# The expert stage of an attention and mixture-of-experts kernel: work order from a list scheduler, low parts of the weights on VectorE, threshold products on the whole array

## The chip, the cores and the metric

The kernel runs on one core of one Trainium2 chip. The metric is the device time of one execution in microseconds (us); the kernel before has a median of 897.88 us over three runs (896.49 to 899.35). The engines are named as the profile names them: PE is TensorE (PEld its weight loads), DVE is VectorE, ACT is ScalarE, POOL is GpSimd, and SP is the engine that issues most DMAs.

## The reference

Linear attention over 8 batches, 8 heads, 576 positions of 64 features feeds a mixture of eight experts over all 4,608 tokens of 512 features. Only the second half matters here:

```python
def _moe_ref(x, w_gate, w1, w2):
    N, D = x.shape; E = w_gate.shape[1]; cap = N // E          # 4608, 512, 8, 576
    logits = x @ w_gate
    order = np.argsort(-logits.flatten())
    # walk all (token, expert) pairs from the highest logit down: a token goes to
    # the first expert that still has room (cap tokens each)
    ...
    for e in range(E):
        mask = assigned == e
        h = np.maximum(x[mask] @ w1[e], 0.0)                   # [576,512] @ [512,1024]
        out[mask] = h @ w2[e]                                  # [576,1024] @ [1024,512]
```

## The kernel before, in words

**Two stages.** The attention stage fills DRAM with the token rows (`xs`) and SBUF with the logits (`L`). Its order comes from a list scheduler, class `Plan`: each piece of work is added with an engine, a duration, a due time and the pieces it needs, and `order()` repeatedly takes the piece that can start first. The change does not alter what the attention stage puts into it. The expert stage, function `moe`, follows.

**Routing.** For the expert that fills up next, `routing(r)` finds which of the eight it is and the 576 tokens that it takes. It fixes the cut-off logit digit by digit. A digit is a chain between DVE and PE: DVE compares every token with 32 or 64 thresholds (`cmp`, L549, bf16), PE counts per expert (L563, nine or eighteen small products of 128 rows), DVE picks the counts (`mm`, `dd`, L564 and L566), PE sums them with `Q` (L568, a product of 32 or 64 columns), DVE tests them against the capacity (`fl`, L571), PE spreads the flags with a matrix of ones (L573, a product over 32 or 64 rows), and DVE reads off the digit and forms the next remainder (`ch`, `cc`, L574 and L578). Six digits make a threshold. Then the expert's number `ei` is known, the taken tokens are ranked (L605, L606) and put into a table (L628, L633, L652), from which `idx`, the list of rows, is written (L654 to L657). At last the logits of what was taken are struck out (L661 to L669). The next expert's `prep` (L465 to L492) needs those logits. So the routing of eight experts is one long chain. Expert 0's routing stands in front of all matmuls; the later ones run beside the experts' matmuls. Expert 7's has no digits, since it gets what is left.

**An expert.** POOL gathers its 576 token rows with five indirect DMAs (`gather`, L675). PE transposes them (L710); ACT copies the result as the high part `xh` (L711) and DVE forms the low part `xl` (L702). All large products are made of three products of rounded 32-bit numbers: high with high, high with low, low with high. The weights come as eight raw chunks of 128x1024 (`wraw`, DMAs on SP), ACT rounds each to its high part (L692), and POOL subtracts it to get the low part (`w1l`, `w2l`, L693; one single chunk of the first expert is done on DVE). Layer 1 (`l1`, L729) is 16 groups of 12 products of 272 or 304 columns; ACT and DVE split each into `fh` and `fl`. Layer 2 (`l2`) is four blocks of 24 products of 512 columns (L747) and a last block of 64 tokens straight from the raw 32-bit weights, which uses only 64 columns of the array (L756). ACT copies each block and POOL scatters it to the output (L760, L761).

**What sets the order.** The expert stage is written out by generators. `l1w` and `l2w` yield after every few products, `run` counts a model time, and `rstep` puts the next step of the routing in when its due time, set by constants such as `lat0`, `latd` and `slack`, has come. The weight chunks and the transposes of the next expert hang at fixed places in those loops. Each engine then works through its own row in order, and an instruction that waits for another engine holds up all that stand behind it in its row.

Of the kernel before, what the change touches and what calls it, by code (L numbers as in the profile page):

```python
# [17 lines left out]
class Plan:  # L18
# [3 lines left out]
    SEM=40.  # L22
    def __init__(self,stay=0.): self.t=[]; self.by={}; self.stay=stay
    def add(self,name,eng,dur,due,fn,deps=(),lat=0.,mode=None,slot=None,frees=(),after=0.):

        x=dict(name=name,eng=eng,dur=dur,due=due,fn=fn,deps=list(deps),lat=lat,mode=mode,slot=slot or (),frees=frees,after=after,n=len(self.t))
        self.t.append(x); self.by[name]=x
    def order(self):
# [7 lines left out]
        while left:  # L36
            best=None; horizon={}
            cand={}
            for x in left:
# [29 lines left out]
            s,x=pick; e=x['eng']
            if e=='PE':  # L70
                if mode[0] not in (None,x['mode']): s+=95.
                if mode[0]!=x['mode'] or s>free.get(e,0.)+1.: s+=100. if x['mode']=='A' else 50.
                mode[0]=x['mode']
            x['start']=s; free[e]=s+x['dur']; x['end']=s+x['dur']+x['lat']
# [307 lines left out]
def moe_consts(rp, nc, C, L, MC, cfg={}):  # L382
# [45 lines left out]
    for n in (2,4):  # L428
        ir=ident.rearrange('p (k i) -> p k i',i=n)
        m=rp.tile([128,n,8],F32,name=f'msk{n}'); q=rp.tile([128,128//n],F32R,name=f'Q{n}')  # L430
# [4 lines left out]
        with nc.allow_low_precision(reason='zeros and ones'): V.tensor_reduce(q.rearrange('p (k o) -> p k o',o=1),ir,axis=AX.X,op=OP.max)  # L435
# [4 lines left out]
    for i in range(2): V.tensor_copy(dup[:,i,:],Q[2])  # L440
# [69 lines left out]
def moe(ctx, tc, nc, L, xs, w1, w2, out, C, MC, R0, cfg={}):  # L510
# [17 lines left out]
    def routing(r):  # L528
# [3 lines left out]
        if not last:  # L532
            R=R0 if r==0 else state()
            if r:
                for x in prep(R,0,NT): yield x
            dg,OH=R['dg'],R['OH']
            c=dg[:,0]; lat=cfg.get('lat0',1.2)
            for i,(sh,bits) in enumerate(DIG):
# [15 lines left out]
                yield lat+.9*K/32  # L554
# [5 lines left out]
                else:  # L560
                    p=rps([128,n,8])
                    for g in range(NT//n):
                        PE.matmul(p,cmp[:,g].rearrange('p k i -> p (k i)'),OH[:,g*n:g*n+n,:],start=g==0,stop=g==NT//n-1)  # L563
                    mm=S([128,n,8],f'mm{n}'); V.tensor_mul(mm,p,msk[n])  # L564
                    dd=S([128,8,1],'dd',F32R)
                    with nc.allow_low_precision(reason='whole numbers under 2**13'): V.tensor_reduce(dd,mm.rearrange('p i e -> p e i'),axis=AX.X,op=OP.add)  # L566
                    yield cfg.get('lq',.9)
                    p=rps([K,8]); PE.matmul(p,Q[n],dd[:,:,0],start=True,stop=True)  # L568
# [3 lines left out]
                yield cfg.get('lo',.6)  # L572
                p=rps([128,8]); PE.matmul(p,ones[0:K],fl,start=True,stop=True)  # L573
# [4 lines left out]
                V.scalar_tensor_tensor(c2,c,ch,dg[:,i+1],op0=OP.subtract,op1=OP.add); c=c2  # L578

# [23 lines left out]
        yield cfg.get('latr',1.6) if not last else cfg.get('lat7',1.5)  # L603
        p=rps([128,2])
        PE.matmul(p,tri,tot,start=True,stop=False)  # L605
        PE.matmul(p[:,1:2],low,tot[:,0:1],start=False,stop=True)  # L606
        off=S([128,2],'off'); V.tensor_copy(off,p)
# [8 lines left out]
        yield -1.3  # L616
# [6 lines left out]
        yield -.9  # L623
# [6 lines left out]
        yield cfg.get('latc',1.6)  # L630
        p=rps([128,9,2,2])
        for g in range(18):
            PE.matmul(p,lo[:,g].rearrange('p k i -> p (k i)'),hv[:,g],start=g==0,stop=g==17)  # L633
        idx=S([128,6,1],'idx',I32,b=3)
        if wide:

            pb=S([128,9,2,2],'pb',BF); V.tensor_copy(pb,p)
            yield cfg.get('lm',.9)
# [5 lines left out]
        else:  # L644
# [14 lines left out]
        if not last:  # L659
            yield -.4  # L660
# [10 lines left out]
    def gather(r):  # L671
        xg=fp.tile([128,5,Dm],F32,name='xg',bufs=cfg.get('bxg',1))
        T['xg',r]=xg
        for b,(o,n) in enumerate(BL):
            G.indirect_dma_start(out=xg[0:n,b,:],out_offset=None,in_=xs,in_offset=bass.IndirectOffsetOnAxis(ap=T['idx',r][0:n,b,:],axis=0))  # L675
    W={}
    def wreg(r):
        W['e',r]=nc.sync.value_load(T['ei',r][0:1,0:1],min_val=0,max_val=E-1)
    def wraw(name,r,c):
        e=W['e',r]; src=w1 if name=='w1' else w2  # L680
        raw=fp.tile([128,4,256] if name=='w1' else [128,2,512],F32,name='raw'+name,bufs=4)
        if name=='w1':
            s=src[ds(e,1)].rearrange('o (k p) f -> p (o k) f',p=128)[:,:,256*c:256*c+256]
        else:
            s=src[ds(e,1)].rearrange('o (k p) f -> p (o k) f',p=128)[:,2*c:2*c+2,:]
        nc.sync.dma_start(raw,s)
        W[name,r,c]=raw
    def wconv(name,r,c,eng=None):
        raw=W[name,r,c]
        h=fp.tile(list(raw.shape),F32R,name=name+'h',bufs=4)  # L690
        l=fp.tile(list(raw.shape),F32R,name=name+'l',bufs=4)
        A.copy(h,raw)  # L692
        (eng or G).tensor_sub(l,raw,h)  # L693
        W[name,r,c]=(h,l,raw)
    def wchunk(name,r,c): wraw(name,r,c); wconv(name,r,c)
    SC=[]
    LQ=[]
    def lag(t,f,*a,**k): LQ.append((st['now']+t,st['lab'],f,a,k))
    def flush(t):
        while LQ and LQ[0][0]<=t:  # L700
            _,lab,f,a,k=LQ.pop(0)
            f(*a,**k)  # L702
    def xt(r,lg=None):
        lg=cfg.get('lgx',.9) if lg is None else lg
        xh=fp.tile([128,4,cap],F32R,name='xh',bufs=1); xl=fp.tile([128,4,cap],F32R,name='xl',bufs=1)
        T['xt',r]=(xh,xl)
        for b,(o,n) in enumerate(BL):
            p=ps.tile([128,4,128],F32,name='h',bufs=cfg.get('hb',4))
            for k in range(4):
                PE.transpose(p[:,k,0:n],T['xg',r][0:n,b,128*k:128*k+128],ident[0:n,0:n])  # L710
            A.copy(xh[:,:,o:o+n],p[:,:,0:n])  # L711
            lag(lg,V.tensor_sub,xl[:,:,o:o+n],p[:,:,0:n],xh[:,:,o:o+n])
            yield .45
    def l1(r,so=False):
        if not so: flush(1e9)
        xh,xl=T['xt',r]
        hh=fp.tile([128,8,512],F32R,name='fh',bufs=1); hl=fp.tile([128,8,512],F32R,name='fl',bufs=1)
        hf=fp.tile([128,8,cap-512],F32,name='ff',bufs=1)
        T['h',r]=(hh,hl,hf)
        SP=(0,cfg.get('hc',288),cap)  # L720
        for i in range(16):
                f,s=(i%8,i//8) if so else (i//2,i%2)
                c,o=f//2,(f%2)*128
                w1h,w1l,_=W['w1',r,c]
                p=ps.tile([128,4,128],F32,name='h',bufs=cfg.get('hb',4))
                o1,o2=SP[s:s+2]; p=p.rearrange('p a b -> p (a b)')[:,0:o2-o1]
                n=0
                for xx,ws,k in [(xh,ws,k) for k in range(4) for ws in (w1h,w1l)]+[(xl,w1h,k) for k in range(4)]:
                    PE.matmul(p,ws[:,k,o:o+128],xx[:,k,o1:o2],start=n==0,stop=n==11); n+=1  # L729
                    if n in (3,6,9): yield .365  # L730
                m1=min(o2,512)-o1
# [164 lines left out]
```

## Time and profile before

| | |
|---|---|
| median of the runs | 897.88 us |
| the profiled execution | 900.97 us, of which the span from its first to its last instruction is 899.1 us |
| mean granted TensorE clock | 0.976 |
| PE busy over the span | 844.9 us (94%) |
| DVE busy | 591.6 us (66%) |
| POOL busy | 425.0 us (47%) |
| ACT busy | 387.1 us (43%) |
| bytes moved by DMA | 91.63 MB |

The first transpose of expert 0 starts at 399.49 us, so the attention stage and the first routing take some 400 us and the expert stage the other 500. A time line row reads: start, duration, engine, line, operation, what it writes and reads, shape, count, and in brackets how long the engine had been idle before it and what ended that idle time. Consecutive matmuls overlap, so what one costs is the distance between two starts, not the duration.

### The profile page before, as it was taken

The numbers are of one execution on the slowest core, as the hardware profiler recorded it, in microseconds if no ns is written. First come the engines' busy times: TensorE is split into PE (matmuls) and PEld (weight loads), VectorE is DVE, ScalarE is ACT, GpSimd is POOL, SyncE is SP. The second block draws the span as 40 slices with busy tenths as digits, with TensorE's granted clock in tenths as the row PEclk, the third lists the DMA queues.
The fourth block names the chain that finished last, engine by engine and source line by source line (L and its number), as shares of the span: only waits on it lengthen the run. The fifth ranks groups of instructions, "written<-read, shape, count | busy, mean of one in ns | idle before, by whom it ended". The sixth has DMA issues, their size and how long they took to land.

```text
span 899.1 us, 20953 instructions
## 1 busy us (share of the span) xinstructions
PE 844.9 (94%) x8332; PEld 728.9 (81%) x8332; DVE 591.6 (66%) x1655; ACT 387.1 (43%) x836; POOL 425.0 (47%) x399
## 2 busy tenths in 40 slices
PE   7999999999999999658989999999999899999995
PEld 5788888888888888657768869869779788798894
DVE  7798898889889988667765665655656645520210
ACT  3556666666566666322323324333333233343420
POOL 2945655555454444043273463553642734665321
PEclk9999999999999999759999999999999999999998
DMA  9534444444444400142133241440531331550301
GB/s 193 128 89 112 104 116 106 116 108 108 106 107 108 107 28 28 55 147 94 61 121 112 97 128 71 131 162 2 170 124 55 127 112 60 185 196 35 112 12 41
DMA packets 73520, 91.63 MB, mean 102 GB/s; under 512 B 5280, under 2 KB 56512, under 8 KB 73424
## 3 DMA queue, kind: packets, MB, share of 16 engines
q1 hardware_dynamic: 67328, 71.32, 28.4%
q0 software_dynamic: 6096, 18.98, 6.3%
q8 instruction: 66, 1.08, 0.5%
q14 instruction: 30, 0.25, 0.1%
HBM read 71.40 MB, written 18.87 MB: 100 GB/s over the span
## 4 chain that ended last, share of the span: by engine, by line
PE 69%; DVE 21%; issue 4%; POOL 2%; DMA 1%; ACT 1%; POOLq 0%; DVEq 0%; ACTq 0%
PE h L729 22%; PE y L747 11%; PE g L300 6%; PE kv L192 6%; PE y L756 3%; DVE cmp L628 2%; PE g L275 2%; PE h L710 2%; DVE cmp L549 2%; DVE qm L268 1%; DVE kt L175 1%; DVE qtt L271 1%; PE g L263 1%; PE g L265 1%; PE rps L563 1%
## 5 line engine op out<-in xcount | busy, mean ns | idle before, releaser
L729 PE MATMUL h<-xh,w1h 128*128 128x272 f32 (+1 forms) x512 | 145.2, 305 | 0.0
L729 PE MATMUL h<-xh,w1l 128*128 128x272 f32 (+1 forms) x512 | 141.5, 298 | 0.0
L693 POOL TENSOR_TENSOR w2l<-raww,w2h 128x1024 fp32r<-128x1024 f32 x32 | 76.4, 2390 | 116.3 <-ACT w2h L692 89.6
L732 ACT ACTIVATE fh<-h 128x272 fp32r<-128x272 f32 (+1 forms) x128 | 49.2, 384 | 146.1 <-PE h L729 144.1
L205 POOL TENSOR_TENSOR ks<-kP 128x512 f32<-128x512 f32 x32 | 41.0, 1280 | 132.7 <-issue 131.3
L747 PE MATMUL y<-w2h,fh 128*128 128x512 f32 x256 | 102.5, 401 | 0.0
L747 PE MATMUL y<-w2l,fh 128*128 128x512 f32 x256 | 101.8, 398 | 0.0
L747 PE MATMUL y<-w2h,fl 128*128 128x512 f32 x256 | 101.4, 396 | 0.0
L693 POOL TENSOR_TENSOR w1l<-raww,w1h 128x1024 fp32r<-128x1024 f32 x31 | 75.3, 2432 | 50.9 <-ACT w1h L692 50.3
L729 PEld LDWEIGHTS h<-xh,w1h 128*128 128x128 f32 x512 | 96.9, 189 | 0.9
L729 PEld LDWEIGHTS h<-xh,w1l 128*128 128x128 f32 x512 | 97.1, 190 | 0.1
L729 PE MATMUL h<-xl,w1h 128*128 128x272 f32 (+1 forms) x512 | 91.9, 298 | 4.3 <-DVE xl L702 4.3
L300 PEld LDWEIGHTS g<-kz,qP 128*64 128x64 f32 x2304 | 82.3, 136 | 11.0 <-DVE qtt L271 3.7
L278 ACT ACTIVATE qP<-g 128x512 f32<-128x512 f32 (+1 forms) x160 | 79.8, 553 | 16.8 <-PE g L275 15.0
L206 POOL TENSOR_TENSOR ks<-ks,kP 128x512 f32<-128x512 f32 x64 | 81.9, 1279 | 9.9 <-ACT kP L180 5.2
L300 PE MATMUL g<-kz,qP 128*64 128x73 f32 x2304 | 84.9, 227 | 0.1
L702 DVE SCALAR_TENSOR_TENSOR fl<-h,fh 128x272 fp32r<-128x272 f32 (+1 forms) x128 | 51.9, 417 | 46.2 <-ACT ff L734 27.2
L729 PEld LDWEIGHTS h<-xl,w1h 128*128 128x128 f32 x512 | 75.5, 189 | 4.7 <-DVE xl L702 4.5
L761 POOL DMA_INDIRECT out_dram<-ysb,idx x40 | 40.1, 1002 | 80.8 <-ACT ysb L749 51.1
L192 PE MATMUL kv<-kP,vi 128*64 128x256 f32 x512 | 68.1, 383 | 0.9 <-ACT kP L180 0.9
L749 ACT COPY ysb<-y 128x512 f32<-128x512 f32 x32 | 18.8, 586 | 112.6 <-issue 68.5
L179 ACT ACTIVATE kP<-kt 128x512 f32<-128x512 f32 (+1 forms) x80 | 47.2, 589 | 40.3 <-DVE kt L175 40.2
(201 smaller groups left out, 1995.8 us busy)
## 6 DMA issues: line engine op xcount, KB each, us to landing
raww<-in_moe_w_dram SPq DMA_DIRECT2D x64, 512.0 KB, 5.5
qi<-in_q_dram SPq DMA_DIRECT2D x32, 288.0 KB, 5.4
xs<-xp SPq DMA_DIRECT2D x16, 576.0 KB, 3.6
ki<-in_k_dram SPq DMA_DIRECT2D x32, 160.0 KB, 3.8
vi<-in_v_dram SPq DMA_DIRECT2D x32, 160.0 KB, 5.4
ki<-in_k_dram SPq DMA_DIRECT2D x32, 128.0 KB, 3.8
vi<-in_v_dram SPq DMA_DIRECT2D x32, 128.0 KB, 5.2
xg<-xs,idx POOLq DMA_INDIRECT x40, 3.6
```

The costliest lines, as they stand in the source:

```text
L179: A.activation(kP[:,:,0:128],t,AF.Exp)
L192: PE.matmul(T['kvps',u][64*half:64*half+64,a,:],v_[:,a,s_,:] if s_!=4 else VZ[:,a,half,:],kP[:,b,:],start=b in (0,5),stop=s_==4,skip_group ...
L205: if i==0: G.tensor_add(ks[:,:,a],X(0),X(1))
L206: elif i<3: G.tensor_add(ks[:,:,a],ks[:,:,a],X(i+1))
L278: for fh in range(2): A.activation(qP[:,fh,0:2*n],X['T'][:,0:2*n],AF.Exp,scale=1.0-2*fh)
L300: PE.matmul(p[64*ab:64*ab+64,j-j0,:],T['qP',u,jj][:,fh,o,64*ab:64*ab+64],kz[:,fh,ab,:],start=fh==0,stop=fh==1)
L693: (eng or G).tensor_sub(l,raw,h)
L702: f(*a,**k)
L729: PE.matmul(p,ws[:,k,o:o+128],xx[:,k,o1:o2],start=n==0,stop=n==11); n+=1
L732: A.activation(hh[:,f,o1:o1+m1],p[:,0:m1],AF.Relu)
L747: PE.matmul(p,hx[:,f,o:o+128],ws[:,f%2,:],start=n==0,stop=n==23); n+=1
L761: st=G.indirect_dma_start(out=ov,out_offset=bass.IndirectOffsetOnAxis(ap=iv,axis=0),in_=yv,in_offset=None)
```

## The change

It has three parts.

1. **Order.** The generators `gather`, `wraw`, `wconv`, `xt`, `l1`, `l2` and the stepping code (`stream`, `rstep`, `run`, `lag`) go. Everything from expert 0's strike-out of logits on is added to a second `Plan` in small pieces: routing split into single steps between DVE and PE (`steps`), layer 1 in pieces of three products, layer 2 in pieces of two, the weight conversions, gathers, transposes and scatters one by one. `Plan` learns `lock` (DVE pieces with SBUF inputs and POOL's DMAs are not planned on top of each other) and `seq`. Due times come from the table `MOE`. The rotating buffers get fixed numbers.
2. **Low parts.** All 64 weight chunks have their low part formed on DVE, in two halves of 128x512 each. POOL has no arithmetic left in this stage beyond clearing the one-element `spacer`.
3. **Threshold products.** `Q` is padded with zero columns to 128, so L568's product writes all 128 rows; the flags `fl` are then 128 rows high, and the product with ones (L573) is over 128 rows. Expert 0's routing keeps 32 and 64.

```diff
-    def add(self,name,eng,dur,due,fn,deps=(),lat=0.,mode=None,slot=None,frees=(),after=0.):
+    def add(self,name,eng,dur,due,fn,deps=(),lat=0.,mode=None,slot=None,frees=(),after=0.,lock=False,seq=None):
...
+            if x['lock'] and e=='DVE': s=max(s,free.get('POOL',0.))
+            if x['lock'] and e=='POOL': s=max(s,self.dl)
...
-        m=rp.tile([128,n,8],F32,name=f'msk{n}'); q=rp.tile([128,128//n],F32R,name=f'Q{n}')
+        m=rp.tile([128,n,8],F32,name=f'msk{n}'); q=rp.tile([128,128],F32R,name=f'Q{n}')
...
+        V.tensor_scalar(q[:,128//n:],C['jp'][:,128//n:],0.0,None,op0=OP.mult)
...
-                    p=rps([K,8]); PE.matmul(p,Q[n],dd[:,:,0],start=True,stop=True)
-                fl=S([K,8],f'fl{K}',BF)
+                    p=rps([128,8]); PE.matmul(p,Q[n],dd[:,:,0],start=True,stop=True)
+                    yield
+                KR=K if wide else 128
+                fl=S([KR,8],f'fl{KR}',BF)
...
-                p=rps([128,8]); PE.matmul(p,ones[0:K],fl,start=True,stop=True)
+                p=rps([128,8]); PE.matmul(p,ones[0:KR],fl,start=True,stop=True)
...
-        A.copy(h,raw)
-        (eng or G).tensor_sub(l,raw,h)
...
+                def lo(y,nm=nm,r=r,c=c,q=0):
+                    h,l,raw=W[nm,r,c]
+                    if nm=='w1': V.tensor_sub(l[:,2*q:2*q+2],raw[:,2*q:2*q+2],h[:,2*q:2*q+2])
+                    else: V.tensor_sub(l[:,q],raw[:,q],h[:,q])
...
+                add((nm+'h',r,c),'ACT',950.,due,hi,dep,slot=((f'{nm}hl{c}',1,(nm+'hl',r,c)),)+(((f'r1{c}',1,('r1',r,c)),) if r==0 and nm=='w1' else ()),after=af)
+                for q in range(2):
+                    add((nm+'l',r,c,q),'DVE',DV(512),due+.9,lambda y,f=lo,q=q: f(y,q=q),[(nm+'h',r,c)],frees=(('r'+k,r,c),),lock=True)
...
+            add(('ga',r,bb),'POOL',1250.,b+d['g']+.1*bb if r else bb*.1,ga,[('idx',r)] if r else [],slot=(('xg',1,('xg',r)),) if bb==0 else (),frees=(('idx',r),) if r else (),lat=2600.,lock=True,seq=('ga',r,bb-1) if bb else None)
...
+                add(('p',r,f,s,q),'PE',3*(N1/2.4+12),due+.4*q,lambda y,g=mms,q=q: g(y,q=q),dep,mode='A',slot=sl,frees=(('xt',r),('w1hl',r,c)) if q==3 else ())
...
+    for x in P.order(): x['fn'](x)
+
+MOE = {'TE': 57.0, 'stay': -0.21, 'sem': 100.0, 'ch': -48.63, 'cp': 1.04, 'w1': 35.54, 'w2': 0.73, 'xt': 27.55, 'hl': 2.26, 'g': -1.95, 'y': -0.56, 'w20': 41.07, 'c1': 0.0, 'cp1': 0.14, 'wp': 150.45}
```

How the rows of three engines change is shown at three places, first before, then now. Line numbers now are those of the changed kernel: low parts L759 and L760, `xl` L778, `cmp` L553, gathers L771, scatters L858, `Q` L574, ones L581, layer 1 L800, the 64-token block L844.

DVE's row at the start of the expert stage, behind expert 0's strike-out, where expert 1's `prep` (m to OH) and first comparison `cmp` stand among expert 0's `xl`. Before:

```order
L693 TENSOR_TENSOR w1l<-raww_6493,w1h 128x1024
L702 TENSOR_TENSOR xl<-h,xh 128x4x128
L465 TENSOR_REDUCE m<-L 128x36
L702 TENSOR_TENSOR xl<-h,xh 128x4x128
L471 TENSOR_SCALAR s_6653<-m 128x36
L472 TENSOR_SCALAR s_6654<-m 128x36
L473 TENSOR_SCALAR s_6657<-m 128x36
L702 TENSOR_TENSOR xl<-h,xh 128x4x128
L476 TENSOR_TENSOR scb<-L,m 128x288
```

Now, from the second `xl` to the first comparison:

```order
L778 TENSOR_TENSOR xl<-h_6644,xh 128x4x128
L485 TENSOR_TENSOR scb<-scb,e_f 128x288
L486 TENSOR_SCALAR dg<-di 128x36
L488 TENSOR_SCALAR di<-s_6652 128x36 x5
L759 TENSOR_TENSOR w1l_6616<-raww_6497,w1h_6615 128x512
L494 TENSOR_REDUCE sm<-scb 128x36
L490 TENSOR_TENSOR dg<-di,scl 128x180
L759 TENSOR_TENSOR w1l_6616<-raww_6497,w1h_6615 128x512
L497 TENSOR_TENSOR OH<-scb,sm 128x288
L553 TENSOR_TENSOR cmp_6706<-dg,kt_432 128x1152
L778 TENSOR_TENSOR xl<-h_6660,xh 128x4x128
L778 TENSOR_TENSOR xl<-h_6685,xh 128x4x128
```

The halves of chunk 1 moved from POOL to a place in front of the comparison, and the comparison moved in front of the third and fourth `xl`.

POOL's row in the middle of the stage, one expert's gathers and scatters (`xg`, `out_dram`) with the low parts of the weights. Before:

```order
L693 TENSOR_TENSOR w1l<-raww_9555,w1h 128x1024
L675 DMA xg<-xs,idx 128x512 x4
L675 DMA xg<-xs,idx 64x512
L760 MEMSET spacer 1x1
L761 DMA out_dram<-ysb,idx 4608x512
L693 TENSOR_TENSOR w1l<-raww_9669,w1h 128x1024
L760 MEMSET spacer 1x1
L761 DMA out_dram<-ysb,idx 4608x512
L693 TENSOR_TENSOR w1l<-raww_9718,w1h 128x1024
```

Now:

```order
L771 DMA xg<-xs,idx 128x512 x2
L857 MEMSET spacer 1x1
L858 DMA out_dram<-ysb,idx 4608x512
L771 DMA xg<-xs,idx 128x512 x2
L857 MEMSET spacer 1x1
L858 DMA out_dram<-ysb,idx 4608x512
L771 DMA xg<-xs,idx 64x512
L857 MEMSET spacer 1x1
```

The subtractions are gone from POOL, and scatters now stand between the gathers.

PE's row around an expert's 64-token block (`y<-raww,ff`), with the routing steps and transposes (`h<-ident,xg`) that stand in it. Before:

```order
L756 MATMUL y<-raww_9098,ff 64x256 x2
L568 MATMUL rps<-dd,Q_725 32x8
L756 MATMUL y<-raww_9098,ff 64x256 x2
L756 MATMUL y<-raww_9191,ff 64x256 x4
L573 LDWEIGHTS onesb
L573 MATMUL rps<-fl_9801,onesb 128x8
L756 MATMUL y<-raww_9295,ff 64x256 x2
L710 MATMUL h<-ident,xg 128x128 x4
L756 MATMUL y<-raww_9295,ff 64x256 x2
L756 MATMUL y<-raww_9399,ff 64x256 x4
L710 MATMUL h<-ident,xg 128x128 x4
```

Now:

```order
L844 MATMUL y_9848<-raww_9095,ff 64x256 x4
L844 MATMUL y_9848<-raww_9127,ff 64x256 x4
L844 MATMUL y_9848<-raww_9154,ff 64x256 x4
L844 MATMUL y_9848<-raww_9178,ff 64x256 x4
L574 MATMUL rps<-dd,Q_726 128x8
L800 MATMUL h_9877<-xh,w1h_9586 128x272
```

The block is whole; the transposes went up among layer 2's products and the routing steps to both sides of the block.

More of the change, by code (lines that the diff above doesn't have):

```diff
@@ L73, in order @@
                 mode[0]=x['mode']
+            if x['lock'] and e=='DVE': self.dl=s+x['dur']
             x['start']=s; free[e]=s+x['dur']; x['end']=s+x['dur']+x['lat']
@@ L533, in routing @@
             R=R0 if r==0 else state()
[L534 to L535 removed]
+            if r: yield from prep(R,0,NT)
             dg,OH=R['dg'],R['OH']
@@ L602, in routing @@
         V.tensor_copy(tot,scn[:,:,NT-1])
-        yield cfg.get('latr',1.6) if not last else cfg.get('lat7',1.5)
+        yield
         p=rps([128,2])
@@ L688, in wconv @@
[L688 to L713, printed above, removed]
@@ new lines, in moe, with add @@
+    d=dict(TE=57.,stay=.3,sem=100.,ch=-50.,cp=1.2,w1=20.,w2=-6.,xt=30.,hl=1.2,g=-4.,y=1.,w20=12.,c1=0.,cp1=.5,wp=60.)
+    d.update(MOE)
+    P=Plan(d['stay']*1e3); P.SEM=d['sem']; P.wp=d['wp']
+    DV=lambda n: 55.+1.03*n
+    SC=[]
+    def add(name,eng,dur,due,fn,deps=(),mode=None,slot=(),frees=(),lat=None,after=0.,lock=False,seq=None):
+        P.add(name,eng,dur,due,fn,deps,lat={'PE':170.,'DVE':95.,'ACT':100.,'POOL':30.,'SP':0.}[eng] if lat is None else lat,mode=mode,slot=slot,frees=frees,after=after,lock=lock,seq=seq)
@@ new lines, in steps @@
+    def steps(last):
+        z=[]
+        if not last:
+            z+=[('DVE',460),('DVE',300),('DVE',570),('DVE',930),('DVE',600),('DVE',370+750)]
+            for i,(sh,bits) in enumerate(DIG):
+                two=KW[i]==64
+                if i: z+=[('DVE',820*(2 if two else 1))]
+                z+=[('PE',(450 if two else 230)+130,'A'),('DVE',400),('PE',110,'A'),('DVE',160),('PE',110,'A')]
+                if i<ND-1: z+=[('DVE',450)]
+        z+=[('DVE',980 if not last else 600,'ei'),('DVE',1100),('PE',120,'A'),('DVE',1450),('DVE',850),('DVE',1400),('PE',600,'A'),('DVE',430),('PE',140,'A'),('DVE',1000)]
+        if not last: z+=[('DVE',1750)]
+        return z
@@ new lines, in up0, with f @@
+    def up0(x):
+        for _ in it0: pass
+    add(('up',0),'DVE',1750.,2.,up0,lock=True)
+    prev=('up',0)
+    for r in range(1,E):
+        it=routing(r)
+        z=steps(r==E-1)
+        t=d['TE']*(r-1)+(d['ch'] if r>1 else d['c1'])
+        ni=len(z)-(2 if r<E-1 else 1)
+        for i,x in enumerate(z):
+            def f(y,it=it): next(it,None)
+            nm=('idx',r) if i==ni else ('up',r) if i>ni else ('rt',r,i)
+            if len(x)>2 and x[2]=='ei':
+                nm=('ei',r)
+            sl=(('idx',3,('idx',r)),) if i==ni else ()
+            add(nm,x[0],float(x[1]),t+i*d['cp' if r>1 else 'cp1'],f,(prev,),mode=x[2] if x[0]=='PE' else None,slot=sl,lock=x[0]=='DVE')
+            prev=nm
@@ L784, in moe @@
-    st.update(g=-1,xt=-1,lab='')
-    def tryg():
-        while st['g']<min(st['done'],st['xt']+1):
-            st['g']+=1; gather(st['g'])
-    def need(k,r):
-        while st[k]<r: rstep()
-    def run(it,label,cap_r):
-        st['lab']=label
-        for d in it:
-            st['now']+=d; flush(st['now'])
-            while not st['over'] and st['due']<=st['now'] and st['done']<cap_r: rstep()
-    need('done',0)
-    for c in range(4): wconv('w1',0,c,V if c<cfg.get('w0v',2) else G)
-    run(iter([1.0]*cfg.get('pre',6)),'pre',1)
```

280 lines of the change are left out of this document (146 added, 134 removed).

## The prediction

> **What bounds the kernel now.** I read the page first, then the expert stage alone, then what PE waits for in it. The page's totals by engine:
>
> ```profile
> PE 844.9 (94%) x8332; PEld 728.9 (81%) x8332; DVE 591.6 (66%) x1655; ACT 387.1 (43%) x836; POOL 425.0 (47%) x399
> ```
>
> The stage from the first transpose to the last matmul, in the view of busy time by windows (length, then PE, PEld, DVE, ACT, POOL, clock, DMA share and rate):
>
> ```profile
> 399.49:889.70 490.21, 470.69 (x3371) 402.08 (x3371) 254.66 (x729) 156.59 (x332) 230.15 (x178) 0.99 0.30 102
> ```
>
> PE is the bound: 470.7 of 490.2 us busy at clock 0.99. DVE is busy for half the stage. So only two things pay: PE's waits, and time that PE loses between its own instructions. Its waits in the same stretch (total, times, longest):
>
> ```profile
> PE rps L563 <- DVE cmp L549: 11.0, 9, 2.2
> PE h L729 <- DVE xl L702: 4.3, 1, 4.3
> PE rps L633 <- DVE cmp L628: 3.9, 5, 1.2
> ```
>
> All 15 end with DVE, which is half idle. The time line of DVE and that of POOL say why DVE is late:
>
> ```profile
> 402.83 4.88 DVE L471 TENSOR_SCALAR s<-m 128x36 int32<-128x36 int32 x1
> ...
> 646.64 0.74 DVE L549 TENSOR_TENSOR cmp<-dg,kt 128x1152 bf16<-128x1152 bf16 x1
> ...
> 652.59 3.55 DVE L549 TENSOR_TENSOR cmp<-cc,kt 128x1152 bf16<-128x1152 bf16 x1
> ```
>
> ```profile
> 400.68 6.98 POOL L693 TENSOR_TENSOR w1l<-raww,w1h 128x1024 fp32r<-128x1024 f32 x3
> ...
> 645.35 0.95 POOL L675 DMA_INDIRECT xg<-xs,idx  x1 [0.30 <-issue]
> 646.61 1.56 POOL L675 DMA_INDIRECT xg<-xs,idx  x1 [0.31 <-issue]
> ...
> 653.15 2.37 POOL L693 TENSOR_TENSOR w1l<-raww,w1h 128x1024 fp32r<-128x1024 f32 x1
> ```
>
> The same comparison takes 0.74 us alone and 3.55 us when a subtraction on POOL overlaps it; it ends 0.62 us after POOL's (656.14 against 655.52). The 36-column shift of 4.88 us ends when POOL's three subtractions end (407.71 against 407.66). A DVE operation of this kind stands still while POOL subtracts, and PE behind it.
>
> **The waits that go.** What such a wait costs PE is more than its idle time:
>
> ```profile
> 403.97 0.29 PE L729 MATMUL h<-xh,w1l 128*128 128x272 f32 x1
> 408.54 0.76 PE L729 MATMUL h<-xl,w1h 128*128 128x272 f32 x4 [4.28 <-DVE xl L702]
> ...
> 410.34 0.43 PE L729 MATMUL h<-xh,w1h 128*128 128x272 f32 x1
> 410.57 0.43 PE L729 MATMUL h<-xh,w1l 128*128 128x272 f32 x1
> ...
> 437.58 0.71 PE L729 MATMUL h<-xl,w1h 128*128 128x304 f32 x4
> 439.15 0.39 PE L563 MATMUL rps<-OH,cmp 128*128 128x16 bf16 x9 [0.86 <-DVE cmp L549]
> ```
>
> Four products of 304 columns need 4 x 0.14 = 0.55, so 439.15 is 1.02 late where the bracket says 0.86: 0.16 of restart each, 2.4 over 15. After the long wait, starts are 0.23 apart against 0.125 for the same shape elsewhere; for some 13 products that is 1.4. With 11.0 + 4.3 + 3.9 = 19.2 idle, POOL's arithmetic costs PE 19.2 + 2.4 + 1.4 = 23.0. The change removes all of that arithmetic.
>
> Next late at the front is DVE itself. The price of a half there:
>
> ```profile
> 396.00 1.22 DVE L693 TENSOR_TENSOR w1l<-raww,w1h 128x1024 fp32r<-128x1024 f32 x1
> 401.26 0.69 DVE L702 TENSOR_TENSOR xl<-h,xh 128x512 fp32r<-128x512 f32 x1 [4.04 <-ACT xh L711]
> 401.87 0.44 DVE L465 TENSOR_REDUCE m<-L 128x36 f32<-128x288 f32 x1
> ...
> 407.81 0.68 DVE L702 TENSOR_TENSOR xl<-h,xh 128x512 fp32r<-128x512 f32 x1
> ...
> 412.20 0.74 DVE L549 TENSOR_TENSOR cmp<-dg,kt 128x1152 bf16<-128x1152 bf16 x1
> ```
>
> A whole chunk on DVE took 1.22; a 512-column subtraction blocks its follower for 0.61 (401.26 to 401.87), so I take 0.61 for a half and nothing for the cut. [...]
>
> At the front the order puts expert 1's comparison on PE behind 12 products, where PE arrives at about 404.3 (403.97 plus a few tenths). DVE's row from the first `xl` at 401.26 to that comparison holds what 407.81 to 412.94 holds now, 5.13, less a `fl`, an `xl` of 64 tokens and a copy (0.74), plus two halves (1.22): 5.6, so it ends at 406.9. PE waits 2.6 and 0.16; whether its pace drops again I leave at half, 0.7. Given back: 3.5. Net of the waits: **19.5**.
>
> **The product with ones.** `Q` (L568) already has 128 rows in, ones (L573) 32 or 64:
>
> ```profile
> 434.67 0.30 PE L729 MATMUL h<-xh,w1h 128*128 128x304 f32 x1
> 434.81 0.17 PE L568 MATMUL rps<-dd,Q 128*64 128x8 f32 x1
> 434.83 0.39 PE L729 MATMUL h<-xh,w1l 128*128 128x304 f32 x1
> 435.06 0.30 PE L729 MATMUL h<-xh,w1h 128*128 128x304 f32 x1
> 435.20 0.30 PE L729 MATMUL h<-xh,w1l 128*128 128x304 f32 x1
> 435.43 0.18 PE L573 MATMUL rps<-fl,onesb 64*128 64x8 bf16 x1
> 435.53 0.41 PE L729 MATMUL h<-xh,w1h 128*128 128x304 f32 x1
> 435.78 0.30 PE L729 MATMUL h<-xh,w1l 128*128 128x304 f32 x1
> ```
>
> Against a pace of 0.14, `Q` costs 0.02 and 0.09 in the distance after it: 0.11. Ones costs 0.09 before it, 0.10, and 0.11 after it: 0.30. With 128 rows ones should cost what `Q` costs: 0.19 less, 36 times (six digits of six experts), less five that stand in a 64-token block: **5.9** (nothing, if the 0.30 is not due to the rows). `Q` with 128 columns: nothing to 0.1 each; the weight load hides behind the product before it.
>
> **The 64-token block.** One transpose group inside it:
>
> ```profile
> 660.25 0.65 PE L756 MATMUL y<-raww,ff 128*64 128x256 f32 x4
> 660.84 0.66 PE L710 MATMUL h<-ident,xg 128*128 128x128 f32 x4
> 661.43 1.52 PE L756 MATMUL y<-raww,ff 128*64 128x256 f32 x12
> 662.87 0.66 PE L710 MATMUL h<-ident,xg 128*128 128x128 f32 x4
> ```
>
> Twelve products take 1.44 and four 0.59, so 0.106 each and 0.165 to leave the block; entering costs the rest of 0.59 over four transposes of 0.11, 0.15. An interruption is 0.3, three in each of seven blocks: 6. The order now keeps the block whole or cuts it once, but three more transpose groups an expert cut layer 2, at a `Q`'s 0.11: 2.3 back. I take **3** (0 to 4).
>
> **What is added.** 126 halves x 0.61 = 77 us on DVE. Its 254.7 less some 20 of standing still plus 77 is 312 of 466 us: two thirds, and not the bound. But its row is in order, and a routing step behind a half waits for it. Two rows for the shortest link, products to `Q`:
>
> ```profile
> 440.32 0.16 DVE L564 TENSOR_TENSOR mm<-rps,msk 128x16 f32<-128x16 f32 x1
> 440.51 0.17 DVE L566 TENSOR_REDUCE dd<-mm 128x8 fp32r<-128x16 f32 x1
> ```
>
> `mm` to the end of `dd` is 0.36; with the product's own 0.17 to 0.18 and two hand-overs of 0.05, some 0.65 from the last counting product. PE's row now has mostly six layer-1 products there, 0.75 to 0.83 and a restart of 0.09: it fits by 0.2, and not where a half or an `fl` stands ahead of `mm`. There are 108 such links (three in each of 36 digits). At worst each waits a fifth of a half, 0.12: 13. At best none does. I take **-3**, near the lower end, because most halves stand behind `dd` or `fl`, where PE does not wait for what follows.
>
> The gathers: POOL is free to issue them the moment `idx` is written, but a DVE half stands right behind `idx`, and 646.61 against 645.35 shows a gather 0.6 longer when a DVE comparison starts just behind it. The first transposes stand 26 layer-2 products behind the table step, 5.9 us; I take **-1** (0 to -3.5, half a us for seven experts).
>
> The weights: SP issues their DMAs once `ei` is read, ACT casts, DVE subtracts. How long that takes:
>
> ```profile
> 690.58 0.15 DVE L591 TENSOR_SCALAR ei<-mx 128x1 int32<-128x1 f32 x1
> ```
>
> ```profile
> 695.09 1.06 ACT L692 CAST w1h<-raww 128x1024 fp32r<-128x1024 f32 x1 [1.84 <-DMA raww<-in_moe_w_dram]
> ```
>
> 4.4 to the landing and 1.1 for the cast, 5.5. The first half now stands on DVE right ahead of `idx`; PE's row has 21 + 30 layer-1 and 8 layer-2 products in between, over 8 us. It is hidden by 2.5. ACT's work is the same, and the scatters that now stand among the gathers wait for blocks that end earlier than the next transposes are due: nothing for both.
>
> **The sum.** 19.5 + 5.9 + 3 - 3 - 1 = 24.4. The span goes from 899.1 to 874.7, this execution's time from 900.97 to 876.6. It lay 3.1 above the median of 897.88, so I predict **873.5 us**.
>
> **The rivals.**
> - *The links tighten* (0.18): DVE at two thirds meets PE at many of the 108 links, 13 to 18 us come back: 883 to 892. For it: gaps of 0.75 where before they were 1.25 to 2. Against it: the links of 2 to 3 us to the comparisons stay long.
> - *Held gathers* (0.07): every gather waits for a DVE operation, five times 0.6, in seven experts: 21 back, about 894. For it: 646.61. Against it: 645.35 and its like, and that only the first of five is needed at once. [...]
> - *Weights late, slower* (0.08): the half ahead of `idx` waits for its weights, and with it `idx`, the gathers, the transposes and layer 1. It decides from the point where landing and cast take 8 us instead of 5.5; at 12 us seven experts lose 4 each, 28, and PE's pace drops as after 408.54: 903 to 910. Against it: 1.84 of wait in the row above, DMA share 0.30.
> - *Ones is no cheaper* (0.04): 5.9 less, 879.
> - The forecast itself: 0.63.
>
> **Range and chances.** Low: no new waits and the block at 4, 24.4 + 3 + 1 + 1, and 0.7 of pace, 868; small waits under 0.3 us that I did not count reach it to 862. High: the links at 13 and the gathers at 3.5 give 886; 888. Beyond it lie the held gathers, the late weights and the end of the tight links, under 0.2. A measurement of this kernel can tell 0.3% from no change, 2.7 us. Faster: 0.63 + 0.17 + 0.04 and half of the held gathers, 0.87; the same 0.05; slower 0.08.
>
> **What would show it.** Right: no DVE comparison over 1.5 us; PE's waits for `cmp` under 5; ones followed by 0.03 instead of 0.10; a stage of 465 us. Wrong: PE waiting for `dd`, `fl` or `xg` by more than 10 us in all, DVE rows that wait for weights, or a granted clock under 0.97.

## The result, and the profile after

The changed kernel takes 875.5 us (median of 4 runs, 874.43 to 876.95) against 898.49 for the kernel before: a ratio of 0.9748 (95% interval 0.9726 to 0.9771). The forecast was 873.5. The profiled execution took 876.95, its span 875.2. Over all chips of this record single runs of the kernel before lie between 893 and 907 us and those of the changed one only between 874 and 878, so below kernels are set beside others of the same chip where these exist, or stages of traces are compared.

The page's totals by engine, then the expert stage from its first transpose to its last matmul (length, then PE, PEld, DVE, ACT, POOL, clock, DMA share and rate):

```profile
PE 834.5 (95%) x8332; PEld 731.1 (84%) x8332; DVE 620.8 (71%) x1784; ACT 388.1 (44%) x836; POOL 274.5 (31%) x336
```

```profile
403.42:865.85 462.43, 459.51 (x3371) 401.43 (x3371) 282.41 (x851) 157.08 (x332) 79.23 (x116) 0.99 0.33 108
```

The stage is 27.8 us shorter (490.2 before): 16.6 of that is idle time of PE (19.5 before, 2.9 now) and 11.2 is time in which PE counted as busy. POOL's 230 us of work in the stage are down to 79. But the stage starts at 403.42 where it started at 399.49: 3.9 us were lost before it, in a part of which the prediction says nothing. The mean granted clock is 0.978 (0.976 before). What PE still waits for in the stage:

```profile
PE h L776 <- PE h L866: 1.8, 1, 1.8
PE rps L567 <- DVE cmp L553: 1.8, 1, 1.8
PE h L800 <- ACT xh L777: 0.9, 1, 0.9
PE h L776 <- DVE xl L778: 0.2, 1, 0.2
```

That is the whole list, and all of it lies in the first ten microseconds; its first row is the wait of the very first transpose. There were 17 waits before and there are 4 now, and none for `dd`, `fl` or `xg` behind the start. The 42 comparisons on a remainder (`cmp<-cc`) on DVE, first before, then after (busy time, mean ns of one, idle time before them):

```profile
L549 DVE TENSOR_TENSOR cmp<-cc,kt 128x1152 bf16<-128x1152 bf16 x42 | 41.4, 1009 | 1.0
```

```profile
L553 DVE TENSOR_TENSOR cmp<-cc,kt 128x1152 bf16<-128x1152 bf16 x42 | 30.6, 753 | 0.4
```

They are back at the 0.75 that one takes alone, and the longest comparison of the stage takes 0.76 where the longest took 3.62. A product with ones on PE's time line after:

```profile
435.44 0.30 PE L800 MATMUL h<-xh,w1l 128*128 128x304 f32 x1
435.57 0.30 PE L800 MATMUL h<-xh,w1h 128*128 128x304 f32 x1
435.72 0.18 PE L581 MATMUL rps<-fl,onesb 128*128 128x8 bf16 x1
435.75 0.39 PE L800 MATMUL h<-xh,w1l 128*128 128x304 f32 x1
435.98 0.30 PE L800 MATMUL h<-xh,w1h 128*128 128x304 f32 x1
```

The product with ones is followed after 0.03 us and no longer after 0.10, as forecast.

Where the stage's 27.8 us came from can be added up from the trace: for each pair of neighbouring large products on PE, the distance of their starts less the pace of that shape (0.125, 0.138, 0.227, 0.109, 0.107), grouped by what stands between them.

| between the large products | before, us | after, us | gain |
|---|---|---|---|
| 36 groups of counting products (L563, now L567) | 24.7 | 14.5 | 10.3 |
| 7 groups of table products (L633, now L644) | 8.1 | 3.3 | 4.8 |
| nothing, products of one kind (the long wait for `xl` among them) | 23.7 | 18.3 | 5.4 |
| 36 products with ones | 7.8 | 1.8 | 6.0 |
| 36 products with `Q` | 1.9 | 2.6 | -0.6 |
| into, within and out of the 64-token block | 3.2 | 0.8 | 2.4 |
| transposes to layers and back, the rest | 1.0 | 1.3 | -0.4 |

### The profile page after: what moved, and what is told of

The parts are those of the page before. It is cut to its first block, busy times and chain, and to the rows that moved or that the text cites. A ratio compares the mean times of both kernels' runs of the same rounds, so it can differ in the third digit from the quotient of the medians.

```text
span 875.2 us, 20970 instructions
## 1 busy us (share of the span) xinstructions
PE 834.5 (95%) x8332; PEld 731.1 (84%) x8332; DVE 620.8 (71%) x1784; ACT 388.1 (44%) x836; POOL 274.5 (31%) x336
## 4 chain that ended last, share of the span: by engine, by line
PE 66%; DVE 15%; issue 12%; POOL 4%; DMA 2%; SPq 1%; ACT 0%; POOLq 0%; DVEq 0%; ACTq 0%
PE h L800 19%; PE y L829 15%; PE g L304 6%; PE kv L196 6%; PE y L844 2%; PE g L279 2%; DVE qtt L275 2%; DVE qm L272 2%; DMA vi<-in_v_dram 2%; PE h L776 2%; DVE kt L179 1%; DVE km L176 1%; PE rps L567 1%; POOL out_dram L858 1%; PE g L267 1%
## 5 line engine op out<-in xcount | busy, mean ns | idle before, releaser
L800 PE MATMUL h<-xh,w1h 128*128 128x272 f32 (+1 forms) x512 | 145.6, 305 | 0.9 <-ACT xh L777 0.9
L800 PE MATMUL h<-xh,w1l 128*128 128x304 f32 (+1 forms) x512 | 143.6, 300 | 0.0
L858 POOL DMA_INDIRECT out_dram<-ysb,idx x40 | 40.7, 1017 | 208.8 <-ACT ysb L852 205.2
L800 PEld LDWEIGHTS h<-xh,w1h 128*128 128x128 f32 x512 | 96.9, 190 | 2.7 <-ACT xh L777 1.3
L800 PEld LDWEIGHTS h<-xh,w1l 128*128 128x128 f32 x512 | 97.1, 190 | 0.0
L771 POOL DMA_INDIRECT xg<-xs,idx x40 | 40.1, 1004 | 178.5 <-issue 141.7
L800 PE MATMUL h<-xl,w1h 128*128 128x272 f32 (+1 forms) x512 | 92.1, 299 | 0.0
L800 PEld LDWEIGHTS h<-xl,w1h 128*128 128x128 f32 x512 | 76.2, 190 | 0.0
L196 PE MATMUL kv<-kP,vi 128*64 128x256 f32 x512 | 66.0, 383 | 0.8 <-ACT kP L184 0.8
L852 ACT COPY ysb<-y 128x512 f32<-128x512 f32 (+1 forms) x40 | 21.8, 545 | 100.2 <-PE y L829 65.2
L778 DVE TENSOR_TENSOR xl<-h,xh 128x512 fp32r<-128x512 f32 (+1 forms) x40 | 25.4, 638 | 43.9 <-ACT xh L777 37.8
```

The lines of the kernel that those rows point to most:

```text
L196: PE.matmul(T['kvps',u][64*half:64*half+64,a,:],v_[:,a,s_,:] if s_!=4 else VZ[:,a,half,:],kP[:,b,:],start=b in (0,5),stop=s_==4,skip_group ...
L771: G.indirect_dma_start(out=T['xg',r][0:n,bb,:],out_offset=None,in_=xs,in_offset=bass.IndirectOffsetOnAxis(ap=T['idx',r][0:n,bb,:],axis=0))
L858: st=G.indirect_dma_start(out=ov,out_offset=bass.IndirectOffsetOnAxis(ap=iv,axis=0),in_=yv,in_offset=None)
```

## The experiments

The changed kernel itself ran twice more as a yardstick. 

> The changed kernel once more, as the yardstick of the three others on this chip. 874 to 877 us, span about 2 less. The expert stage (first transpose to last matmul) 462 to 463 us long, its start at 403 to 404.

 

> The changed kernel as the yardstick of the two others on this chip: 874 to 877 us.

 Measured: 875.82 both times; the stage starts at 402.29 and 403.85 and is 462.3 long from first start to last start in both.

**Low parts back on GpSimd, in the new order.**

```
-if nm=='w1': V.tensor_sub(l[:,2*q:2*q+2],raw[:,2*q:2*q+2],h[:,2*q:2*q+2])
-else: V.tensor_sub(l[:,q],raw[:,q],h[:,q])
+if nm=='w1': G.tensor_sub(l[:,2*q:2*q+2],raw[:,2*q:2*q+2],h[:,2*q:2*q+2])
+else: G.tensor_sub(l[:,q],raw[:,q],h[:,q])
```

> The changed kernel with the subtractions of the low parts back on GpSimd, as halves, everything else and the order on every engine kept. Theory: VectorE's operations on SBUF stand still again during some 150 us of GpSimd subtractions, comparisons take up to 2 us and more, and TensorE's waits come back: 15 to 25 us, so 890 to 900 us. Rival: the gain is the new order's, which puts routing steps early enough; then comparisons lengthen but TensorE still does not wait, and the time stays at 875 to 879.

Measured 912.9 (910.9 to 913.24): 37 more than the changed kernel on the same chip, more than the 15 to 25 of theory, against the rival's 875 to 879, and slower than every run of the kernel before there (896.31 to 907.24). PE's waits for the comparisons:

```profile
PE rps L567 <- DVE cmp L553: 23.1, 16, 6.3
```

The longest of them on POOL, DVE and PE (start, duration, ...):

```profile
485.52 7.40 POOL L760 TENSOR_TENSOR w2l<-raww,w2h 128x512 fp32r<-128x512 f32 x6
```

```profile
485.64 7.34 DVE L587 SCALAR_TENSOR_TENSOR cc<-cc,ch,dg 128x36 bf16<-128x36 bf16 x1
493.01 0.76 DVE L553 TENSOR_TENSOR cmp<-cc,kt 128x1152 bf16<-128x1152 bf16 x1
```

```profile
487.20 0.29 PE L800 MATMUL h<-xh,w1l 128*128 128x272 f32 x1
493.82 0.42 PE L567 MATMUL rps<-OH,cmp 128*128 128x32 bf16 x9 [6.34 <-DVE cmp L553]
```

A step of 36 columns, 0.26 us alone, stands still for 7.34: it does not get in between six subtractions in a row, and ends 0.06 after the last. From within this wait on the granted clock is down to half for 6.7 us (stretch, length, busy times, then clock, DMA share and rate):

```profile
490.70:497.40 6.70, 3.58 (x23) 3.40 (x24) 3.60 (x5) 1.33 (x2) 2.38 (x3) 0.50 0.00 0
```

So a long wait came with slow products as well, which may be why theory was too low. The new order without the low parts on VectorE is no gain: GpSimd's arithmetic costs it more than it cost the old one. That this is because it sets the steps closer together is likely, but not shown; the halves in a row on GpSimd differ from the whole chunks of before too.

**Low parts on VectorE, in the old order.** One line of the kernel before:

```
-        (eng or G).tensor_sub(l,raw,h)
+        V.tensor_sub(l,raw,h)
```

> The kernel before the change with nothing but the engine of the low parts changed: all 64 subtractions on VectorE, as whole chunks, in the old order. Theory: what GpSimd's arithmetic cost TensorE in the old order goes, 23 us; some of it comes back at the start (three chunks of 1.22 stand before the first low part of the tokens) and where a chunk of 1.22 stands before a routing step, 4 to 10; the stage goes from 490 to 470 to 477, the time to 880 to 887. Rival: the gain needs the new order, since in the old one chunks of 1.22 take the place of the subtractions that held VectorE up; the stage stays above 484 and the time above 892.

Measured 925.35 (922.11 to 927.48), against 902.11 for the kernel before on that chip: 23 slower. Both numbers of theory are missed and the rival's side holds, but not for its reason. VectorE's low parts in that run (busy time, mean, then idle time ahead of them and what ended it), then its time line at the table step:

```profile
L693 DVE TENSOR_TENSOR w2l<-raww,w2h 128x1024 fp32r<-128x1024 f32 x32 | 39.2, 1225 | 40.6 <-ACT w2h L692 40.6
L693 DVE TENSOR_TENSOR w1l<-raww,w1h 128x1024 fp32r<-128x1024 f32 x30 | 36.6, 1224 | 56.6 <-ACT w1h L692 56.6
```

```profile
511.17 0.76 DVE L702 SCALAR_TENSOR_TENSOR fl<-h,fh 128x240 fp32r<-128x240 f32 x2
515.78 1.23 DVE L693 TENSOR_TENSOR w1l<-raww,w1h 128x1024 fp32r<-128x1024 f32 x1 [3.85 <-ACT w1h L692]
516.92 0.40 DVE L702 SCALAR_TENSOR_TENSOR fl<-h,fh 128x240 fp32r<-128x240 f32 x1
517.24 0.15 DVE L607 COPY off<-rps 128x2 f32<-128x2 f32 x1
```

VectorE stands idle for 97 us in front of low parts whose high part ACT has not cast yet, here with the table step `off` behind. Of ACT's own waits only 19.7 us are for weights that have not landed; the rest of the 97 is the cast, 1.1 us each, and what stands ahead of it in ACT's row. PE then waits for the table step's comparisons, 20.9 us where it was 3.9. First ACT, then PE:

```profile
ACT w1h L692 <- DMA raww<-in_moe_w_dram: 19.7, 7, 6.0
PE rps L633 <- DVE cmp L628: 20.9, 14, 4.4
```

PE's idle time in the stage grows by 12.4 us only (from 19.5 to 31.9), but it is also busy 12.5 us longer with the same products (483.2 instead of 470.7), at a mean granted clock of 0.96 instead of 0.99 in the stage. On GpSimd such waits, 140 us in the trace of before, held up nobody: no wait of PE there ends with POOL. In the changed kernel the same groups wait 2.2 us for casts:

```profile
L759 DVE TENSOR_TENSOR w1l<-raww,w1h 128x512 fp32r<-128x512 f32 x64 | 42.8, 684 | 1.2 <-ACT w1h L756 1.1
L760 DVE TENSOR_TENSOR w2l<-raww,w2h 128x512 fp32r<-128x512 f32 x64 | 42.5, 685 | 1.8 <-ACT w2h L756 1.1 <-issue 0.5
```

**The old order, with the low parts on VectorE put later.** That this is the reason was then tried: each subtraction goes into a list and is written 7 us of planned time behind its load, or at the latest ahead of the layer that needs it.

```
-        (eng or G).tensor_sub(l,raw,h)
+        if eng: V.tensor_sub(l,raw,h)
+        else: WL.append((st['now']+7.,name,lambda: V.tensor_sub(l,raw,h)))
...
-            st['now']+=d; flush(st['now'])
+            st['now']+=d; flush(st['now']); wflush(st['now'])
...
```

`wflush` writes what has come due.

> The kernel before the change, low parts on VectorE as whole chunks, and each subtraction put into VectorE's row some 7 us of planned TensorE time behind the issue of its chunk's load instead of right at it; loads, casts and TensorE's order as before. Theory: the 27 us that the low parts on VectorE lost in the old order came from its row standing still for weights that had not landed (97 us idle for the casts in that run's trace, 3.85 ahead of a table step); put later, VectorE waits for casts under 15 us, the waits of the table step (20.9) go, and the time is 878 to 890, below the kernel before. Rival: the routing steps of the old order have no room for 1.22 us chunks at all; the time stays above 905.

Measured 880.94 (879.32 to 881.04) against 903.43 on that chip. With the place of the subtractions alone, 23 us more than the kernel before became 22.5 less. The stage is 470.3 long from first start to last start (489.8 before), VectorE waits 8.4 us for casts, and PE waits for VectorE nowhere:

```profile
PE h L715 <- DMA xg<-xs,idx: 3.1, 3, 1.5
PE h L735 <- issue: 0.2, 1, 0.2
```

So the old order with its low parts moved to VectorE, at this distance behind their loads, gains 22.5 us where the changed kernel gained 27.8 on a chip on which the kernel before took almost the same (903.61): four fifths. In the stage it gains 19.5 of 27.8 us. The products with ones are worth 6.0 by the table, and what is left, 2.3, is what the table has for the block. By this sum the new order has no gain of its own in the stage beyond the whole block. The old order with low parts put later and products with ones on 128 rows, which would settle it, was not run.

**Threshold products on 32 or 64 rows again.**

```
-                    p=rps([128,8]); PE.matmul(p,Q[n],dd[:,:,0],start=True,stop=True)
+                    p=rps([K,8]); PE.matmul(p,Q[n][:,0:K],dd[:,:,0],start=True,stop=True)
...
-                KR=K if wide else 128
+                KR=K
```

> The changed kernel with the threshold products back on 32 or 64 rows and columns, the order on every engine unchanged. Theory: each of 36 products with ones costs 0.16 us more between its neighbours (0.20 against 0.04 in the two traces), so the stage grows by 5.6 and the time to 881 (880 to 882). Rival one: the 0.30 of before was due to the order around it and not to the rows, no difference. Rival two: the products with ones move only the place where TensorE waits, under 2 us.

Measured 881.73 (881.02 to 882.15) against 875.82 on the same chip: 5.9; the stage 5.5 longer (467.8 from first to last start), the groups with ones 7.3 instead of 1.8 us, those with `Q` 2.1 instead of 2.6. Theory holds, and both rivals fall. A product with ones in that run:

```profile
439.56 0.72 PE L800 MATMUL h<-xl,w1h 128*128 128x304 f32 x4
440.21 0.18 PE L581 MATMUL rps<-fl,onesb 64*128 64x8 bf16 x1
440.32 0.50 PE L829 MATMUL y<-w2h,fh 128*128 128x512 f32 x1
```

Again 0.10 ahead of it (four products take 0.55) and 0.11 behind. These are stops on both sides of a product on 64 rows among products on 128; the changed kernel's product on 128 rows (435.72) starts 0.15 behind the one before it, at a pace of 0.14, and is followed after 0.03. What makes TensorE stop there was not shown.

**Every half computed twice.** `lo` writes each half two times, 78 us more for VectorE.

```
+                    for _ in range(2):
...
```

> The changed kernel with every half of the low parts computed twice on VectorE, the order kept: 78 us more on VectorE, whose share of the stage goes from 282 of 462 us to 78%. It tells how near VectorE is to being the bound. By the slack in the trace (of 36 Q products 10 follow their dd by under 0.3 us, of 36 products with ones 7), theory one, the links are close to tight: a half more before some 20 to 40 of 108 links costs 0.3 each, and the front 1.2 to 2.5, together 8 to 15 us. Rival: slack elsewhere takes it up, under 4 us.

Measured 917.95 (917.17 to 920.45), 42 more than the 875.82 that the changed kernel took on two other chips (it did not run on this one); theory had 8 to 15, the rival under 4, and both are wrong. PE now waits where the prediction's rival "the links tighten" had it:

```profile
PE rps L574 <- DVE dd L571: 8.9, 13, 1.0
PE rps L567 <- DVE cmp L553: 8.7, 14, 1.1
PE rps L581 <- DVE fl L579: 6.0, 14, 1.5
PE h L801 <- DVE fl L816: 5.4, 6, 2.2
```

VectorE is busy for 365 of the 505 us then, 72%. It is not full, and still a half costs 0.33 of its 0.61: here the in-order links bound long before the engine's total did. PE's idle time grows by 28 us (from 2.9 to 30.9), and PE is busy 14.8 longer with the same products; three stretches of 3.4 us at half the granted clock that lie behind the start, where the changed kernel has none, are part of that (mean clock of the stage 0.98, there 0.99). I had counted only the places where the measured slack was under 0.3, one link at a time; but a link that comes late probably makes the next one late.

**Whole chunks in the new order.**

```
-                    if nm=='w1': V.tensor_sub(l[:,2*q:2*q+2],raw[:,2*q:2*q+2],h[:,2*q:2*q+2])
-                    else: V.tensor_sub(l[:,q],raw[:,q],h[:,q])
+                    if q==0: V.tensor_sub(l,raw,h)
```

> The changed kernel with each chunk's low part computed whole at the place of its first half (1.22 us there) and nothing at the place of the second; the rest of the order kept. It tells whether the cut into halves pays. Theory: it does, since a routing step or a relu's low part that stands behind the first half comes 0.61 later; doubling all 126 halves cost 42 us or 0.34 each, so 63 first halves that grow cost up to 21, of which the empty second places give some back: 8 to 20 us, 884 to 896. Rival: VectorE's total stays the same and the empty places give it all back, within 3 us of the changed kernel.

Measured 876.27 (875.8 to 876.88) beside 875.82: theory's 8 to 20 us did not come, the rival holds, and the cut into halves brings nothing that can be measured, nor does it cost anything.

**What was lost in the attention stage.** Two suspects: the rule for matmul pieces in `order()`, which the attention stage also uses, and the two operations that fill `Q`'s new columns with zeros (L440). These two stand among the constants that are built in the attention stage, so the change does put something into it. First the rule, for the attention stage alone (`self.pl` is 1 for the expert stage's plan only):

```
-r=max(r,y['end']+self.SEM if e!='PE' or y['eng']!='PE' else y['start']+y['dur'])
+r=max(r,y['end']+self.SEM if e!='PE' or y['eng']!='PE' else (y['start']+y['dur'] if self.pl else y['end']))
...
```

> The changed kernel with the attention stage ordered by the old rule for one piece of matmuls that follows another (ready at the end of the earlier one, latency included, instead of at its start plus its duration); the expert stage keeps the new rule. Theory: the expert stage began 3.9 us later after the change, 0.6 of it by the first load, 3.3 because the rule also reorders the attention stage and makes TensorE wait for VectorE there; so the stage begins at 399.5 to 400.1, stays 462.4 long, and the time is 872 (871.5 to 873). Rival: the later start is chance of one execution, the same time as the changed kernel within 0.1%.

Measured 874.62 (873.18 to 875.73) beside 875.82 (874.65 to 877.55): 1.2 less, a third of what was expected (872), with the runs of the two overlapping. TensorE's order in that stage is the old one again but for two neighbours that changed places, yet the expert stage starts at 402.10, hardly earlier than the 402.29 of the yardstick. So what theory said of the start failed. Of the 2.1 us between the two profiled executions 1.9 lie in the expert stage, which theory had unchanged: 460.8 long instead of 462.7 from the first start to the last end, and 1.6 of these 1.9 arise in its first 100 products on PE. The mean granted clock from 399.7 to 416.7 is 0.90 there, 0.73 in the yardstick; what sets it was not tried. Left is a place at 49 us. VectorE there before, and after:

```profile
48.19 0.28 DVE L435 TENSOR_REDUCE Q<-ident 128x64 fp32r<-128x128 f32 x1
...
48.80 0.47 DVE L433 COPY msk<-ms 128x32 f32<-128x32 f32 x1
49.18 0.54 DVE L155 TENSOR_TENSOR kl<-g,kh 128x384 fp32r<-128x384 f32 x1
```

```profile
48.91 0.28 DVE L439 TENSOR_REDUCE Q<-ident 128x64 fp32r<-128x128 f32 x1
49.10 0.89 DVE L440 TENSOR_SCALAR Q<-jp 128x64 fp32r<-128x64 f32 x1
...
50.31 1.00 DVE L437 COPY msk<-ms 128x32 f32<-128x32 f32 x1
51.23 0.55 DVE L159 TENSOR_TENSOR kl<-g,kh 128x384 fp32r<-128x384 f32 x1
```

From `Q` to `kl` it is 2.32 where it was 0.99, and PE waits for `kl` for 1.76 where it waited 0.42, first before, then after:

```profile
49.78 0.39 PE L167 MATMUL g<-w2h,kh 128*128 128x256 f32 x1 [0.42 <-DVE kl L155]
51.83 0.38 PE L171 MATMUL g<-w2h,kh 128*128 128x256 f32 x1 [1.76 <-DVE kl L159]
```

So the zeros were put behind the last of the constants, alone and together with the old rule:

```
-        V.tensor_scalar(q[:,128//n:],C['jp'][:,128//n:],0.0,None,op0=OP.mult)
...
+    yield
+    for n in (2,4):
+        V.tensor_scalar(Q[n][:,128//n:],C['jp'][:,128//n:],0.0,None,op0=OP.mult)
+        yield
```

> The changed kernel with the two operations that fill the new columns of Q with zeros moved from the middle of the constants to their end; TensorE's order unchanged. Theory: where they stand now they hold up the low parts of k at 49 us, and TensorE's wait for those is 1.8 us instead of 0.4 before the change; moved, the wait is 0.4 again, the expert stage starts 1.4 earlier (401.0 where it was 402.3) and the time falls by 1.4, to 874.4 beside 875.8. Rival: the wait only moves to the next place in the attention stage, no difference (within 0.4 us).

> The zeros late, and the attention stage ordered by the old rule. Theory: both losses in the attention stage are gone and add up, 1.4 and 1.2 to 1.5: 873.0 (872.4 to 873.8), the expert stage starting at about 400. Rival: they overlap, 874.4 as with one of them.

> Zeros late and the attention stage by the old rule, again, beside the changed kernel on one chip. Theory: the two losses in the attention stage, 2.7 to 3.9 us from run to run, are gone, and it is faster than the changed kernel by 3 to 5 us. Rival: the 871.1 of the first time was that chip's, and the two are within 1.5 us.

Measured on one chip, on which the changed kernel did not run: 874.44 (872.22 to 876.14) with the zeros late, 871.13 (870.57 to 872.92) with both, less than the 872.4 to 873.8 expected. On the other: 873.27 (872.03 to 874.0) with both beside 875.82 (874.75 to 877.64) for the changed kernel. PE's wait for `kl` is 0.41 to 0.42 again in all three. The start of the stage with both, in the first run:

```profile
399.71 2.39 PE L779 MATMUL h<-ident,xg 128*128 128x128 f32 x12 [2.17 <-DMA xg<-xs,idx]
```

Both together give back 2.6 us on the one chip where the two ran side by side, short of the 3 to 5 expected, with runs that do not overlap; the stage starts at 399.7 and 400.8, near the 399.5 of before. That makes it the fastest version here. Taking both edits back moved the start from 403.85 to 400.77 on that chip, so they did put it later. But here too the expert stage is shorter than in the yardsticks, 460.4 to 460.8 us instead of 462.7, so that part of what was won comes from its first products and not from the attention stage. How the 2.6 divide between these, rule and zeros, runs with a scatter of 2 to 4 us do not settle.

## Why the prediction was right, point by point

*What bounds the kernel.* Right: PE's waits and the time that it loses between its own instructions were what could be gained, and the stage lost 27.8 us without a change in the products' number.

*Waits that go, net 19.5.* The first three rows of the table give 20.5. The front gave back less: the first comparison of expert 1 makes PE wait 1.8 instead of 2.6, and a cast 0.9 that the sum did not have. The size of the term is right, and the old order with VectorE's low parts put later loses just these waits: its stage is 19.5 us shorter. The drop in PE's pace that the prediction counts after the long wait (0.23 instead of 0.125) goes with a granted clock of 0.50, which it does not name. The stretch before, then the one of the changed kernel and the rest of its stage:

```profile
409.50:412.80 3.30, 3.30 (x17) 3.18 (x15) 3.30 (x15) 0.61 (x2) 0.00 (x0) 0.50 0.00 0
```

```profile
413.40:416.70 3.30, 3.30 (x16) 3.18 (x16) 3.27 (x9) 0.80 (x2) 0.00 (x0) 0.50 0.00 0
416.90:865.85 448.95, 448.91 (x3308) 391.86 (x3306) 270.91 (x818) 152.82 (x324) 78.00 (x113) 1.00 0.33 110
```

The stretch at half clock is as long as before, so the 1.4 of that term did not go there, and the prediction had given back only half of it. The kernel before has another such stretch, from 460.7 to 464.1, that the changed kernel has not.

*What the reason leaves out.* The prediction takes GpSimd's 23.0 for a sum that goes when the engine changes. The new order without the new engine (912.9), and the new engine with each low part right behind its load in the old order (925.4), were both slower than the kernel before. Relief came with a VectorE row in which low parts hardly wait for the casts (8.4 us in the old order with the low parts put later, 2.2 in the new one, 97 where the kernel was slower). The rival "weights late" names that mechanism for the half ahead of `idx`; in the new order it did not come, in the old one it did, though only in part by late landings. How long one hold lasts, the row of 7.34 us shows: VectorE stood still for six of GpSimd's subtractions in a row, not for one of them, which would have been 1.23 (7.40 by six).

*A half at 0.61, nothing for the cut.* Right: two halves in a row are 1.28 to 1.29 in the time lines, one chunk 1.22, and whole chunks gave 876.27. One half takes 0.684 in the trace's mean, but the next instruction starts 0.60 after its start, so two are 1.28 and not 1.37.

*Ones, 5.9.* Right: 6.0 by the table, 5.9 by the time of the experiment. `Q` with 128 columns costs 0.6 in all, near the lower end of what was stated. Its weight load takes 0.19 instead of 0.11 to 0.14, and the trace after has it beside the product before `Q` (the load from 723.93 to 724.12, that product from 723.93 to 724.24, `Q` at 724.07). *The block, 3.* 2.4 by the table, less 0.4 for the extra changes between transposes and layers: about 2.

*New waits at the links, -3, and the gathers, -1.* Both were mis-sized: nothing. The hand-overs that the prediction takes as 0.05 are 0.04 from a product's end to `mm` and 0.06 from a comparison's end to the counting products in the trace of before. PE waits for `dd`, `fl` and gathers not once behind the start. The room is small, though, as the doubled halves show. VectorE's load came out lower than the 312 us of the prediction, 282: by the prediction's own sum (254.7 + 77 - 282.4) some 49 us of standing still went, not 20.

*What failed.* The sum 24.4 was set against the whole span as if nothing ahead of the stage would change. The prediction weighed `Q`'s 128 columns only as a product on PE, and of the scheduler's new rule only what it does in the expert stage. The fill of these columns and the rule's effect on the attention stage made the stage start later, by 3.9 us in the profiled run and 2.8 and 4.4 in the yardsticks. In the stage 27.8 were gained and not 24.4. The two errors cancel: 27.8 - 3.9 = 23.9 off the span, where 24.4 was forecast. That the time came out within 2 us of the forecast is in part luck.

## What to carry to other kernels

Work moved from an engine with little else to do to a busy in-order one takes its waits along: place it behind what it reads, by the time at which the load has landed and the cast is done, or it holds up everything behind it (925 against 881 us with the same instructions, where the kernel before took 902 and 903). When a scheduler's rule or a constant's shape is edited, look at every stage that the rule orders or the constant is built in, not only at the one the edit is meant for. And test the headroom before spending it: at 61% busy VectorE made PE wait nowhere behind the first ten microseconds of the stage, at 72% the kernel was 42 us slower.

## What the runs showed of the hardware

With the low parts on GpSimd, a VectorE step of 36 columns on SBUF operands (`cc`, 0.26 us alone) did not get between queued GpSimd subtractions: it waited for six of them, 7.34 us. The clock that TensorE was granted was 0.50 in some stretches: at the start of the stage, until 402.6 and from 409.5 to 412.9 in the kernel before, until 406.6 and from 413.4 to 416.8 in the changed one; and in versions in which PE waited more, later too, from 460.7 to 464.1 in the kernel before and from 490.7 to 497.4 around the wait of 6.34 us with the low parts on GpSimd. What sets it was not tried. Why the kernel before varies so much more than the changed one from run to run (896.31 to 907.24 on one chip, beside 874.65 to 877.55) was not tried. That kernel has such holds and the changed one has none; but the version with low parts on GpSimd in the new order has more of them (PE waits 23.1 us for comparisons, 11.0 in the kernel before) and stayed between 910.9 and 913.24 in four runs, which speaks against them as the reason.
